# Fewer turns of P, a last stage by seven products, fewer pairs by rows, finer first pairs, and an order read from a table

## The chip, the core and the metric

The kernel runs on one core of a Trainium2 chip. Its metric is the device time of one execution, in microseconds. Five engines run their own instruction streams and wait for each other by semaphores: PE (TensorE: matmul and turns, that is, transposes by a product with the identity), ACT (ScalarE), DVE (VectorE), POOL (GpSimd), and SP, which here only issues DMAs (ACT and POOL issue some too).

## The reference

Inputs are q, k and v of shape (4, 12, 448, 64) and two weight matrices of 768 x 2048 and 2048 x 768, the weights as 64-bit floats. What is computed:

```python
scores = (q @ k.T) / 8, with the upper triangle masked          # 4 batches x 12 heads
attn = softmax(scores)
x = (attn @ v), heads side by side                              # 1792 tokens x 768
h = maximum(x @ w_in, 0)
out = (h * h) @ w_out                                           # 1792 x 768
```

## The kernel before, in words

Two heads of one batch make a **pair**; there are 24. For a pair, q and k are brought to a layout with the 64 head dimensions of both heads along 128 partitions. Most pairs are loaded in 32 x 14 x 32 blocks, eight DMAs for q and k, and DVE transposes 32 x 32 blocks (L403). Pairs 4 to 9 (`ROWS`) are loaded by rows, four DMAs, turned on PE (L389, eight turns a pair), and copied out of PSUM by ACT (L318) or DVE (L399).

The 448 queries of a pair are cut into seven chunks of 64; chunk c sees only its first 64(c+1) keys, so the widths are 64 to 448. Scores (L422) are written with one head in each half of the 128 partitions: each head's product uses 64 rows and 64 columns of the array. DVE adds the mask and takes the extreme of each row (L435), ACT takes the exponential and its sum (L439), DVE inverts the seven sums at once (L515, L516), and POOL or DVE scales P (L448, L450). Then P is turned in 128 x 128 blocks (L462). A chunk whose width is an odd multiple of 64 leaves its last block half empty, filled with zeros at the start (L263); so a pair takes 16 turns in four groups of four, each group one PSUM bank, copied to `pt` by ACT (L318) or DVE (L470). P times V (L482) gives x for two heads. In the names of tiles, a pair's tiles begin with `a` or `b` (even and odd pairs of the first twelve; all later pairs use `a`).

Every large matrix is held as a rounded part and a remainder, and each large product is three matmuls: high x high, high x low, low x high (L679 to L681 and L1098 to L1100 for the first 896 tokens, L860 to L864 and L986 to L988 for the second). The weights come as 64-bit words and are converted by ACT, DVE and POOL.

For the first 896 tokens (pairs 0 to 11), four groups of 512 of the 2048 hidden features go one after another: an h stage (x times w_in, ReLU, square), then an o stage (times w_out). Pairs 12 to 23 are computed meanwhile, and their x goes to memory. The second 896 tokens use a 2 x 2 split of each product with seven block products instead of eight; sums and differences of blocks are prepared by DVE, POOL, ACT and accumulating DMAs that POOL issues. Groups come in the order 0, 3, 2, 1 (`TURNS`). The last o stage, of group 1 (`o_last`), takes all eight block products, as 12 outputs of 12 matmuls; its outputs are added to the sums of earlier groups, transposed by DVE (L1036), and stored. The very last output is added in two parts (`finish`, L1063 to L1078).

The order is set by `Plan`: each `plan.op` has a rank, its engines with estimated times, and what it reads and writes. `emit` runs a list schedule over these estimates and writes the instructions of all engines in that order; `AMENDS` shifts ranks. [...]

Of the kernel before, what the change touches and what calls it, by code (L numbers as in the profile page):

```python
# [20 lines left out]
class Op:  # L21
    __slots__ = ("rank", "ways", "then", "left", "ready", "take", "drop", "lag", "bias")
# [14 lines left out]
class Plan:  # L37

    LAG = {PE: 0.25, ACT: 0.3, DVE: 0.3, POOL: 0.3, DMA: 0.5, DMA2: 0.5}
    ISSUE = 1.4
    BEGIN, BACKLOG = 1.3, 2.5
    FEW = {PE: 0.0, ACT: 0.5, DVE: 1.0, POOL: 0.0, DMA: 0.0, DMA2: 0.0}
    MANY = {PE: 0.0, ACT: 0.0, DVE: 0.3, POOL: 0.0, DMA: 0.0, DMA2: 0.0}

    def __init__(self):  # L50
# [21 lines left out]
    def op(self, rank, ways, reads=(), writes=(), after=(), take=None, drop=(), clear=(), lag=0.0):  # L72
        o = Op()
        o.rank, o.ways, o.then, o.ready, o.take, o.drop = rank, ways, [], 0.0, take, drop
        o.lag, o.bias = lag, self.bias
# [24 lines left out]
    def amend(self, table):  # L100
        for first, end, more in table:
            for o in self.ops[first:end]:
                o.rank += more

    def emit(self):
        free = [1.0, 1.9, 3.4, 2.7, 0.7, 0.7]
        ready = [o for o in self.ops if o.left == 0]
        order, port, net = [], 0.0, 0.0
        while ready:
            best = None  # L110
            for o in ready:
                at = o.ready + (self.ISSUE if o.ways[0][0] >= DMA else 0.0)
                if o.take:
                    h, n = o.take[0], len(o.take)
                    if self.held[h.kind] + n > self.caps[h.kind] or len(self.pools[h.pool]) < n:
                        continue
                    at = max(at, sorted(self.pools[h.pool])[n - 1][0])
                at += o.lag
                if o.ways[0][0] >= DMA:
                    at = max(at, net - self.BACKLOG)  # L120

                w = min(
                    (max(free[w[0]], at, port if shared(w) else 0.0) + w[1] + o.bias[w[0]],
                     max(free[w[0]], at, port if shared(w) else 0.0), i, w[0])
                    for i, w in enumerate(o.ways)
                )
                key = (w[1], o.rank)
                if best is None or key < best[0]:
                    best = (key, o, w)
            _, o, (_, start, i, e) = best  # L130
            ready.remove(o)
            free[e] = end = start + o.ways[i][1]
            if shared(o.ways[i]):
                port = max(port, end)
            if e >= DMA:
                net = max(net, start + self.BEGIN) + o.ways[i][3]
                end = max(end, net)
            order.append((start, len(order), o, i))
# [52 lines left out]
def kernel(  # L191
# [54 lines left out]
    ROWS, RB = range(4, 10), S // NK  # L246
# [4 lines left out]
    class Buffers:  # L251
        def __init__(s, nm, pool):
# [22 lines left out]
    mask = pool.tile([P, S], F32, name="mask")  # L275
# [18 lines left out]
    NX = 9  # L294
    wide = wi_t.rearrange("p i c f -> p (i c f)")
# [12 lines left out]
    for i in range(2):  # L308
        m = mask[i * QC:(i + 1) * QC, S - QC:]
# [34 lines left out]
    def attention(s, n, at):  # L344
# [956 lines left out]
```

## Time and profile before

| | us |
|---|---|
| median of 3 runs (lowest to highest) | 604.77 (604.64 to 605.73) |
| profiled execution, its own time | 606.17 |
| its span, from first to last instruction | 604.3 |
| PE busy | 587.0 (97% of the span) |
| DVE, ACT, POOL busy | 418.8, 361.8, 348.1 |
| mean granted clock of TensorE | 0.999 |

So 1.9 us of the profiled execution lie outside its span. Times below count from the start of the span. "Busy" is the union of an engine's instructions. [...]

### The profile page before, as it was taken

The page shows a single profiled execution, that of the slowest core. Times are in us where ns is not written, and L with a number is a line of the kernel's source. Part 1 is how long each engine was busy: PE and PEld are TensorE (multiplying, and loading weights), DVE is VectorE, ACT ScalarE, POOL GpSimd, SP SyncE. Part 2 cuts the span into 40 slices and gives each one's busy share as a digit, 9 for nine tenths or more (in the row PEclk, how much of TensorE's full clock was granted, in tenths as well). Part 3 has the DMA queues.
Part 4 walks back from the last instruction along what each step waited for, and adds up shares of the span by engine and source line. Part 5 has one row for each costly group of instructions (what it writes and reads, how often), then busy time and mean ns, then how long its engine had stood idle before and what let it go on. Part 6 is the DMA issues. An engine that isn't in the chain of part 4 may idle for free.

```text
span 604.3 us, 11456 instructions
## 1 busy us (share of the span) xinstructions
PE 587.0 (97%) x3766; PEld 513.8 (85%) x3766; DVE 418.8 (69%) x951; ACT 361.8 (60%) x889; POOL 348.1 (58%) x460
## 2 busy tenths in 40 slices
PE   3999999999999999999999999999999999999997
PEld 2677777898988998888898889998999899999996
DVE  4997976366985887775677616688782777777454
ACT  3889997665687656577447543367764573752400
POOL 2574673764585844867557754256685566777000
PEclk9999999999999999999999999999999999999999
DMA  9899745979789888987898759869868746771555
GB/s 148 168 204 179 165 103 116 257 232 329 191 208 315 247 238 217 282 232 226 255 242 259 268 189 263 274 188 238 207 152 163 195 116 135 158 177 41 183 92 93
DMA packets 190652, 120.02 MB, mean 199 GB/s; under 512 B 126016, under 2 KB 178560, under 8 KB 190592
## 3 DMA queue, kind: packets, MB, share of 16 engines
q1 hardware_dynamic: 169488, 107.99, 64.8%
q0 software_dynamic: 6912, 9.44, 10.0%
q10 hardware_dynamic: 14192, 1.85, 1.9%
q8 instruction: 30, 0.49, 0.3%
q14 instruction: 30, 0.25, 0.2%
HBM read 80.71 MB, written 38.54 MB: 197 GB/s over the span
## 4 chain that ended last, share of the span: by engine, by line
PE 90%; DMA 4%; ACT 2%; SPq 2%; issue 1%; DVE 0%; ACTq 0%; DVEq 0%
PE ps L1098 7%; PE ps L679 7%; PE ps L1100 6%; PE ps L1099 6%; PE ps L681 6%; PE ps L680 6%; PE ps L482 6%; PE ps L462 6%; PE ps L986 6%; PE ps L988 6%; PE ps L987 6%; PE ps L422 5%; PE ps L860 5%; PE ps L864 5%; PE ps L862 5%; DMA words<-in_moe_w_in_dram 2%
## 5 line engine op out<-in xcount | busy, mean ns | idle before, releaser
L318 ACT ACTIVATE words<-words 128x384 f32<-128x384 f32 (+3 forms) x140 | 79.8, 597 | 27.9 <-DVE words L321 15.3
L448 POOL TENSOR_SCALAR ap<-ap,asm 128x64 f32<-128x64 f32 (+6 forms) x123 | 74.6, 626 | 30.6 <-DVE asm L516 27.7
L435 DVE CUSTOM_DVE_ANT_0 ps<-ps,mask 128x448 f32<-128x448 f32 (+6 forms) x168 | 68.4, 446 | 19.2 <-PE ps L422 12.9
L1098 PE MATMUL ps<-wo,g 128*128 128x384 f32 x224 | 76.8, 343 | 0.0
L1100 PE MATMUL ps<-wo,g 128*128 128x384 f32 x224 | 75.1, 335 | 0.0
L1099 PE MATMUL ps<-wo,g 128*128 128x384 f32 x224 | 75.0, 335 | 0.0
L679 PE MATMUL ps<-x,wi 128*128 128x448 f32 x192 | 74.1, 386 | 0.6 <-ACT aqt L318 0.6
L681 PE MATMUL ps<-x,wi 128*128 128x448 f32 x192 | 70.3, 366 | 0.0
L680 PE MATMUL ps<-x,wi 128*128 128x448 f32 x192 | 70.3, 366 | 0.0
L439 ACT ACTIVATE ap<-ps,mx 128x448 f32<-128x448 f32 (+6 forms) x126 | 59.2, 487 | 15.0 <-DVE mx L435 11.1
L325 POOL TENSOR_TENSOR wi<-words,wi 128x384 fp32r<-128x384 f32 (+1 forms) x44 | 52.6, 1204 | 11.8 <-ACT wi L318 6.6
L860 PE MATMUL ps<-x,wi 128*128 128x448 f32 x156 | 57.3, 367 | 0.3 <-DMA wi<-wi_split 0.3
L318 ACT ACTIVATE r<-ps 128x448 f32<-128x448 f32 x60 | 32.5, 545 | 41.4 <-PE ps L681 17.5
L862 PE MATMUL ps<-x,wi 128*128 128x448 f32 x156 | 57.2, 367 | 0.0
L864 PE MATMUL ps<-x,wi 128*128 128x448 f32 x156 | 57.2, 367 | 0.0
L986 PE MATMUL ps<-g,wi 128*128 128x448 f32 x153 | 56.0, 366 | 0.3 <-DMA wi<-wo_split 0.3
L987 PE MATMUL ps<-g,wi 128*128 128x448 f32 x153 | 56.0, 366 | 0.0
L988 PE MATMUL ps<-g,wi 128*128 128x448 f32 x153 | 56.0, 366 | 0.0
L331 POOL TENSOR_SCALAR wi<-words 128x384 fp32r<-128x384 f32 (+1 forms) x39 | 26.9, 689 | 46.6 <-DVE words L643 23.0
L640 DVE TENSOR_SCALAR words<-words 128x384 int32<-128x384 int32 (+1 forms) x56 | 30.3, 543 | 23.2 <-ACT words L318 23.1
L321 DVE CUSTOM_DVE_ANT_0 words<-words 128x768 uint16<-128x768 uint16 (+1 forms) x56 | 42.3, 755 | 5.8 <-ACT words L318 3.3
L318 ACT ACTIVATE apt<-ps 128x512 f32<-128x512 f32 x65 | 35.6, 611 | 14.5 <-PE ps L462 14.4
(149 smaller groups left out, 1459.9 us busy)
## 6 DMA issues: line engine op xcount, KB each, us to landing
words<-in_moe_w_in_dram SPq DMA_DIRECT2D x24, 512.0 KB, 5.6
words<-in_moe_w_out_dram SPq DMA_DIRECT2D x32, 384.0 KB, 3.7
wo_split<-wo SPq DMA_DIRECT2D x26, 384.0 KB, 4.8
wi<-wo_split SPq DMA_DIRECT2D x24, 384.0 KB, 4.1
wo_whole<-words SPq DMA_DIRECT2D x32, 192.0 KB, 3.9
wi_split<-wi SPq DMA_DIRECT2D x24, 256.0 KB, 4.0
v<-in_v_dram SPq DMA_DIRECT2D x24, 192.0 KB, 4.1
wi_whole<-words SPq DMA_DIRECT2D x18, 256.0 KB, 4.0
```

The lines of the kernel that those rows point to most:

```text
L318: return (ACT, t_act(n, psum, more), lambda: nc.scalar.activation(dst(), src(), func, **kw))
L679: nc.tensor.matmul(o, w[:, 0], x[:, 0], start=c == 0, stop=False)
L680: nc.tensor.matmul(o, w[:, 0], x[:, 1], start=False, stop=False)
L681: nc.tensor.matmul(o, w[:, 1], x[:, 0], start=False, stop=c == NP - 1)
L860: nc.tensor.matmul(o, w.t[:, 0, c], x[:, 0], start=begin and c == 0, stop=False, skip_group_check=True)
L862: nc.tensor.matmul(o, w.t[:, 0, c], x[:, 1], start=False, stop=False, skip_group_check=True)
L986: nc.tensor.matmul(o, w.t[:, 0, d], g.t[:, 0], start=start, stop=False, skip_group_check=True)
L987: nc.tensor.matmul(o, w.t[:, 0, d], g.t[:, 1], start=False, stop=False, skip_group_check=True)
L988: nc.tensor.matmul(o, w.t[:, 1, d], g.t[:, 0], start=False, stop=stop, skip_group_check=True)
L1098: nc.tensor.matmul(res(), g[:, 0], w[:, 0], start=f == 0, stop=False)
L1099: nc.tensor.matmul(res(), g[:, 0], w[:, 1], start=False, stop=False)
L1100: nc.tensor.matmul(res(), g[:, 1], w[:, 0], start=False, stop=f == GF - 1)
```

## The change

- **Turns.** P of a pair is laid out without gaps, in the chunk order 1, 3, 5, 2, 0, 6, 4 (`ALONG`). The last 64 columns of chunks 2 and 0, and of 6 and 4, then lie side by side and are turned together (`TWINS`): 14 turns a pair instead of 16, in groups of 4, 4, 4 and 2. The group of two is copied out by two instructions of 64 partitions each. In `pt`, the half that such blocks don't fill is set to zero once.
- **Scores of chunk 4.** For this layout its last 64 keys stand first (`FIRST`); its product is written as two matmuls a head, of 256 and 64 columns, and the mask is wider.
- **Rows.** Only pairs 4 and 5 are loaded by rows; 6 to 9 come in blocks, with DVE transposes.
- **First pairs.** Pairs 0 and 1 take their scores in two or three groups with PSUM places of their own, and invert the sums of chunks 0 to 4 and of 5 and 6 apart.
- **Last o stage.** It takes seven block products instead of eight, each of 2 x 3 matmuls on three column blocks. The last pairs of h units therefore make the differences as the other groups do (`plain` is gone), the weights of the stage need the sums that accumulating DMAs build, and the second h pair of group 1 comes before the o stage of group 2. Buffers of x are reused for weights and h once the last h product has read them (`lent_x`).
- **Order.** `emit` no longer plans: each operation has a number in the table `PLACES`, which gives its place in one total order and, by its remainder, the engine.

```diff
+    def emit(self, table):
+        codes = [int(x, 36) for x in table.split()]
+        assert len(codes) == len(self.ops)
+        done = set()
+        for n, (code, o) in enumerate(sorted(zip(codes, self.ops), key=lambda x: x[0])):
+            assert all(d in done for d in o.deps)
...
+            o.ways[code % 3][2]()
...
+                    self.pools[h.pool].append((n + 1,) + h.tile)
+            done.add(o)
...
-    ROWS, RB = range(4, 10), S // NK
+    ROWS, RB = range(4, 6), S // NK
...
+    SOON = {6: (0, 0), 5: (1, 0), 4: (2, 0), 3: (3, 0), 1: (4, 0), 2: (5, 0), 0: (5, 3 * QC)}
+    NEXT = {**PLACE, 0: (3, 7 * QC)}
+    FAST = 2
...
+    ALONG = (1, 3, 5, 2, 0, 6, 4)
+    TWINS = ((2, 0), (6, 4))
+    POFF = {c: sum(CW[x] for x in ALONG[:i]) for i, c in enumerate(ALONG)}
+    FIRST = {4: QC}
...
+    QUADS = (
+        ((5, 0), (6, 0), (5, 1), (6, 1)),
+        ((1, 0), (2, 0), (3, 0), (4, 0)),
+        ((3, 1), (4, 1), (5, 2), (6, 2)),
+        TWINS,
+    )
...
-            for c in range(NQ):
-                if CW[c] < CK[c] * P:
-                    nc.vector.memset(s.p[:, POFF[c] + CW[c]:POFF[c] + CK[c] * P], 0.0)
+            for kc in range(NK):
+                nc.vector.memset(s.pt[QC:, TOFF[kc]:TOFF[kc] + P], 0.0)
...
-                        h = j ^ (PLACE[c][0] & 1)
-                        nc.tensor.matmul(
-                            place(c)[h * QC:(h + 1) * QC], s.qt[mine, c * QC:(c + 1) * QC],
-                            s.kt[mine, :CW[c]], start=True, stop=True, skip_group_check=True)
+                        h = j ^ (place_at[c][0] & 1)
+                        off = FIRST.get(c, 0)
+                        for k0, k1, to in ((0, CW[c] - off, off), (CW[c] - off, CW[c], 0)):
+                            if k0 < k1:
+                                nc.tensor.matmul(
+                                    place(c)[h * QC:(h + 1) * QC, to:to + k1 - k0], s.qt[mine, c * QC:(c + 1) * QC],
+                                    s.kt[mine, k0:k1], start=True, stop=True, skip_group_check=True)
...
-            blocks = TURNED[4 * i:4 * i + 4]
+            blocks = QUADS[i]
+            twins = blocks is TWINS
 
             def go():
                 for n, (c, kc) in enumerate(blocks):
+                    a = POFF[c] + CW[c] - QC if twins else POFF[c] + FIRST.get(c, 0) + kc * P
                     o = QC * (PLACE[c][0] & 1)
-                    nc.tensor.transpose(
-                        ps.t[:, n * P:(n + 1) * P],
-                        s.p[:, POFF[c] + kc * P:POFF[c] + (kc + 1) * P], ident[:, o:o + P])
-            plan.op(at, [(PE, 4 * 0.109, go)], [(nm, "p", c) for c, _ in blocks], [ps],
-                    take=ps, clear=[(nm, "pt", i)], lag=spare(1.6))
-            t = s.pt[:, 4 * i * P:4 * (i + 1) * P]
-            plan.op(at, [
-                on_act(512, lambda: t, lambda: ps.t, True),
-                (DVE, t_dve(512) + 0.05, lambda: nc.vector.tensor_copy(t, ps.t)),
-            ], [ps], [(nm, "pt", i)], drop=[ps])
+                    nc.tensor.transpose(ps.t[:, n * P:(n + 1) * P], s.p[:, a:a + P], ident[:, o:o + P])
+            plan.op(at, [(PE, len(blocks) * 0.109, go)],
+                    [(nm, "p", c) for c in sorted({c for b in blocks for c in (b if twins else b[:1])})], [ps],
+                    take=ps, clear=[(nm, "pt", i, h) for h in range(2)] if twins else [(nm, "pt", i)], lag=spare(1.6))
...
+            if twins:
+                for h in range(2):
+                    copied([(nm, "pt", i, h)], [(b[h], b[h] // 2) for b in blocks],
+                           slice(h * QC, (h + 1) * QC), slice(0, QC))
+            else:
+                copied([(nm, "pt", i)], blocks, slice(None), slice(None))
...
+        if fast:
+            groups = ((6, 5), (4, 3, 2, 1, 0)) if n else ((4, 3), (2, 1, 0), (6, 5))
...
+        for first, end in ((0, 5), (5, NQ))[::-1 if n else 1] if fast else ((0, NQ),):
+            def inverse(sums=s.sm[:, first:end]):
+                nc.vector.tensor_scalar(sums, sums, 1.0e-9, None, op0=ALU.add)
+                nc.vector.reciprocal(sums, sums)
+            keys = [(nm, "sm", c) for c in range(first, end)]
+            plan.op(at, [(DVE, 0.4, inverse) + SHARED], [], keys)
+            for c in range(first, end):
+                normalise(c, keys, at)
...
-        if plain:
-            factor("12", "12", True)
-            return rank
...
+    O_LAST = {"11": ("a", "11"), "12": ("b", "11"), "s2": ("a", "12"), "s1": ("c", "22"),
+              "s3": ("a", "22"), "s4": ("c", "12"), "22": ("a", "21")}
...
-        for k in ("11", "21", "12", "22"):
-            i, j = k
-            for d in range(CB):
-                ps, a = Hold("ps", "os"), o_sum(k, d)
-                rank = o_product(ps, [(W[i + m, u], g7[TURNS[-1], m + j, u]) for m in "12" for u in range(2)],
...
+        bank = {}
+        for d in range(CB):
+            for key, (b, k) in O_LAST.items():
+                begin = key in ("11", "12", "s1")
+                if begin:
+                    bank[b] = Hold("ps", "os")
+                ps, a = bank[b], o_sum(k, d)
+                rank = o_product(ps, [(W[key, u], g7[TURNS[-1], OTHER[key], u]) for u in range(2)],
+                                 d, begin, True, rank, step)
+                if (key, d) == ("22", CB - 1):
+                    finish(ps, k, d, rank)
                     continue
+                plan.op(rank, [on_dve(S, a, lambda ps=ps: ps.t[:, :S], a, ALU.add)], [ps], [("sum", k, d)],
+                        drop=[ps] if key in ("12", "22", "s4") else [])
+                if key in ("12", "22", "s3", "s4"):
+                    put_out(k, d, rank)
...
-        stages += [(a, 0) for a in after] + [(gr, None)] + [(a, 1) for a in after]
-    for gr, u in stages:
+        early_pair = after == TURNS[-1:]
+        stages += [(a, 0) for a in after] + [(a, 1) for a in after if early_pair]
+        stages += [(gr, None)] + [(a, 1) for a in after if not early_pair]
...
-    AMENDS = (
-        (0, 25, 5.5), (25, 31, 9.6), (31, 44, 13.9), (44, 61, 9.6), (61, 62, -25.2), (62, 65, -33.7),
...
-    plan.amend(AMENDS)
+    PLACES = """
+        00c 00l 00o 006 000 003 00i 00f 009 02o 066 07r 07o 00r 00x 02c 02x 030 043 04c 010 01u 020 01f 01x 01i 03r 016
...
```

What the table does to the engines is shown at three places. First PE, at the turns of pair 2 and the scores of pair 4 (`ap` is P of pair 2, `akt` and `aqt` the k and q of pair 4), before:

```order
L462 MATMUL ps_117<-ident,ap 128x128 x4
L462 MATMUL ps_118<-ident,ap 128x128 x4
L462 MATMUL ps_119<-ident,ap 128x128 x4
L462 MATMUL ps_116<-ident,ap 128x128 x4
L422 MATMUL ps_120<-akt,aqt 64x448 x2
L422 MATMUL ps_115<-akt,aqt 64x384 x2
L422 MATMUL ps_115<-akt,aqt 64x64 x2
L422 MATMUL ps_117<-akt,aqt 64x320 x2
L422 MATMUL ps_119<-akt,aqt 64x256 x2
```

and now:

```order
L425 MATMUL ps_117<-ident,ap 128x128 x4
L425 MATMUL ps_119<-ident,ap 128x128 x4
L425 MATMUL ps_113<-ident,ap 128x128 x4
L425 MATMUL ps_118<-ident,ap 128x128 x2
L383 MATMUL ps_116<-akt,aqt 64x448 x2
L383 MATMUL ps_120<-akt,aqt 64x384 x2
L383 MATMUL ps_120<-akt,aqt 64x64 x2
L383 MATMUL ps_114<-akt,aqt 64x256
L383 MATMUL ps_114<-akt,aqt 64x64
L383 MATMUL ps_114<-akt,aqt 64x256
L383 MATMUL ps_114<-akt,aqt 64x64
L383 MATMUL ps_119<-akt,aqt 64x256 x2
```

The last group of turns has two instead of four. Of chunk 4 (320 wide before) the two heads' matmuls no longer stand next to each other: one head's 256 and 64 come ahead of the other head's.

Second DVE, in the first pairs (`bkt` and `bqt` are k and q of pair 1, `asm` the sums of pair 0, ISA with `mask` the extremes of a chunk and `mx` their read-out), before:

```order
L435 ISA ps_115,mx_108<-ps_115,mask 128x320
L435 ISA mx_108 128x1
L435 ISA ps_116,mx_109<-ps_116,mask 128x256
L435 ISA mx_109 128x1
L435 ISA ps_116,mx_110<-ps_116,mask 128x192
L435 ISA mx_110 128x1
L435 ISA ps_115,mx_111<-ps_115,mask 128x128
L435 ISA mx_111 128x1
L403 STREAM_TRANSPOSE bkt<-bk 128x448
L403 STREAM_TRANSPOSE bqt<-bq 128x448
L515 TENSOR_SCALAR asm<-asm 128x7
L516 RECIPROCAL asm<-asm 128x7
```

and now:

```order
L358 STREAM_TRANSPOSE bqt<-bq 128x448
L396 ISA ps_116,mx_108<-ps_116,mask 128x384
L396 ISA mx_108 128x1
L358 STREAM_TRANSPOSE bkt<-bk 128x448
L396 ISA ps_117,mx_109<-ps_117,mask 128x320
L396 ISA mx_109 128x1
L396 ISA ps_115,mx_110<-ps_115,mask 128x448
L396 ISA mx_110 128x1
L503 TENSOR_SCALAR asm<-asm 128x2
L504 RECIPROCAL asm<-asm 128x2
L396 ISA ps_119,mx_111<-ps_119,mask 128x320
L396 ISA mx_111 128x1
```

Pair 1's transposes moved from behind all seven chunks of pair 0 to among them (three narrow chunks stand ahead of this piece), and two sums of pair 0 are inverted before pair 0's chunk of 256, which comes later.

Third DVE at the end of the program (`sb` are sums of outputs, L1036 and now L1034 the transposes ahead of the stores), before:

```order
L321 TENSOR_TENSOR sb_4316<-ps_113,sb_4316 128x448
L1036 STREAM_TRANSPOSE words<-sb_4316 128x448
L321 TENSOR_TENSOR sb_4317<-ps_115,sb_4317 128x448
L1036 STREAM_TRANSPOSE words<-sb_4317 128x448
L321 TENSOR_TENSOR sb_4318<-ps_118,sb_4318 128x256
```

and now:

```order
L276 TENSOR_TENSOR sb_4366<-ps_118,sb_4366 128x448
L276 TENSOR_TENSOR sb_4366<-ps_115,sb_4366 128x448
L1034 STREAM_TRANSPOSE words<-sb_4366 128x448
L276 TENSOR_TENSOR sb_4372<-ps_118,sb_4372 128x448
L1034 STREAM_TRANSPOSE words<-sb_4372 128x448
L276 TENSOR_TENSOR sb_4369<-ps_119,sb_4369 128x448
L276 TENSOR_TENSOR sb_4369<-sb_4369,sa_3859 128x448
L276 TENSOR_TENSOR sb_4369<-ps_118,sb_4369 128x256
```

Each block product of six matmuls now has an addition of its own, where an output of twelve matmuls had one. Of the five block products in this piece the fourth (`sb_4369<-ps_119`) is one of group 2's o stage, and an addition of two sums stands behind it.

## Rows read from the trace of the kernel before

**Rows 1.** The page: PE in 40 slices of the span, busy tenths.

```profile
PE   3999999999999999999999999999999999999997
```

**Rows 2.** Windows: stretch, then busy us (instructions) of PE, PEld, DVE, ACT, POOL; clock, DMA.

```profile
0.00:20.00 20.00, 9.44 (x94) 6.32 (x97) 11.41 (x48) 8.81 (x31) 5.51 (x18) 1.00 0.90 150
20.00:50.00 30.00, 28.13 (x269) 20.59 (x262) 26.95 (x88) 27.13 (x85) 20.08 (x35) 1.00 0.95 189
20.00:106.00 86.00, 84.13 (x787) 62.42 (x781) 70.92 (x237) 76.96 (x237) 52.17 (x93) 1.00 0.75 156
60.00:70.00 10.00, 10.00 (x94) 7.33 (x94) 9.46 (x36) 9.86 (x32) 7.70 (x15) 1.00 0.85 204
350.00:590.00 240.00, 239.43 (x1206) 221.05 (x1205) 160.18 (x261) 117.94 (x235) 128.50 (x149) 1.00 0.68 172
```

**Rows 3.** Waits of PE: line, waited for: us in total, times, longest.

```profile
PE ps L422 <- DVE aqt L403: 7.3, 2, 6.7
```

**Rows 4.** Timeline of PE, 57 to 70 us: start, us, line, tiles, shape, count.

```profile
57.24 0.93 PE L389 MATMUL ps<-ident,rows 112*128 112x112 f32 x8
58.11 1.83 PE L422 MATMUL ps<-bkt,bqt 64*64 64x448 f32 x28
...
65.64 1.75 PE L422 MATMUL ps<-akt,aqt 64*64 64x448 f32 x28
67.32 1.95 PE L482 MATMUL ps<-apt,v 128*64 128x448 f32 x16
```

**Rows 5.** Timeline of PE, first and last of 120 matmuls in the last stage.

```profile
574.80 0.36 PE L986 MATMUL ps<-g,wi 128*128 128x448 f32 x1
...
598.92 0.37 PE L988 MATMUL ps<-g,wi 128*128 128x448 f32 x1
```

**Rows 6.** Timeline of DVE at the end: additions and a transpose.

```profile
596.89 0.62 DVE L321 TENSOR_TENSOR sb<-ps,sb 128x448 f32<-128x448 f32 x1 [1.13 <-PE ps L988]
597.55 0.65 DVE L1036 STREAM_TRANSPOSE words<-sb 128x448 f32<-128x448 f32 x1
```

**Rows 7.** Timeline of PE in narrow windows: scores of one pair, chunk by chunk.

```profile
65.64 0.59 PE L422 MATMUL ps<-akt,aqt 64*64 64x448 f32 x4
66.03 0.58 PE L422 MATMUL ps<-akt,aqt 64*64 64x384 f32 x4
66.45 0.43 PE L422 MATMUL ps<-akt,aqt 64*64 64x320 f32 x4
```

**Rows 8.** Timeline of the first 30 us: pairs 0 and 1.

```profile
6.73 3.27 PE L422 MATMUL ps<-akt,aqt 64*64 64x448 f32 x28 [6.73 <-DVE aqt L403]
8.64 0.63 DVE L435 CUSTOM_DVE_ANT_0 ps<-ps,mask 128x448 f32<-128x448 f32 x1 [1.89 <-PE ps L422]
12.00 0.64 DVE L403 STREAM_TRANSPOSE bkt<-bk 128x448 f32<-128x448 f32 x1
13.22 3.10 PE L422 MATMUL ps<-bkt,bqt 64*64 64x320 f32 x28 [3.22 <-DVE asm L515]
16.25 1.99 PE L462 MATMUL ps<-ident,ap 128*128 128x128 f32 x16
```

**Rows 9.** Groups of DVE by form, 0 to 106 us: count, busy us, mean ns.

```profile
L403 DVE STREAM_TRANSPOSE akt<-ak 128x448 f32<-128x448 f32 x5 | 3.2, 642 | 4.0 <-DMA ak<-in_k_dram 4.0
L470 DVE COPY apt<-ps 128x512 f32<-128x512 f32 x5 | 3.4, 679 | 0.0
L321 DVE TENSOR_TENSOR wi<-words,wi 128x512 fp32r<-128x512 f32 x2 | 1.4, 686 | 0.0
L399 DVE COPY aqt<-ps 128x448 f32<-128x448 f32 x1 | 0.6, 610 | 0.0
L450 DVE TENSOR_SCALAR bp<-bp,bsm 128x384 f32<-128x384 f32 x1 | 0.5, 480 | 0.0
```

**Rows 10.** Timeline at 107 us: POOL and DVE side by side.

```profile
107.68 1.15 POOL L325 TENSOR_TENSOR g<-r,g 128x448 fp32r<-128x448 f32 x1
...
107.86 1.17 DVE L450 TENSOR_SCALAR ap<-ap,asm 128x320 f32<-128x320 f32 x1
```

More of the change, by code (lines that the diff above doesn't have):

```diff
@@ L21 @@
 class Op:
-    __slots__ = ("rank", "ways", "then", "left", "ready", "take", "drop", "lag", "bias")
+    __slots__ = ("rank", "ways", "take", "drop", "deps")
 class Hold:
@@ L37 @@
 class Plan:
[L44 to L48, printed above, removed]
     def __init__(self):
@@ L93, in op @@
                 self.readers.setdefault(k, []).append(o)
-        o.left = len(deps)
-        for d in deps:
-            d.then.append(o)
+        o.deps = deps
         self.ops.append(o)
         return o
[L100 to L138, printed above, removed]
+    def emit(self, table):
[4 more added lines that the diff above has]
+            assert all(d in done for d in o.deps)
             for h in o.take:
@@ L274 @@
     ident = pool.tile([P, 3 * QC], F32, name="ident")
[L275 removed]
+    mask = pool.tile([P, S + CW[4] - QC], F32, name="mask")
     even = Buffers("a", pool)
@@ L486, in times_v @@
             plan.op(at, [(PE, 0.2 + 4 * sum((S - kc * P) / 2400 for kc in range(NK)), go)],
-                    [(vr, kc) for kc in range(NK)] + [(nm, "pt", i) for i in range(len(TURNED) // 4)], [av], take=av, drop=[vr],
+                    [(vr, kc) for kc in range(NK)] + KEYS, [av], take=av, drop=[vr],
                     lag=spare(1.0))
@@ L865, in go @@
                                      skip_group_check=True)
-                plan.op(rank, [(PE, 3 * t_mm(S), go)],
-                        [(w, 0), (w, 1)] + [(("x7", OTHER[key], c), i) for i in range(2)], [ps],
-                        take=ps if begin and c == 0 else None, drop=[w])
+                used.setdefault(OTHER[key], []).append(plan.op(
+                    rank, [(PE, 3 * t_mm(S), go)],
+                    [(w, 0), (w, 1)] + [(("x7", OTHER[key], c), i) for i in range(2)], [ps],
+                    take=ps if begin and c == 0 else None, drop=[w]))
                 rank += step
@@ L946, in o_parts @@
     def o_parts(gr, rank, last):
-        W, Z, gate = {}, {}, list(ahead)
+        W, Z, gate, order = {}, {}, list(ahead), tuple(O_LAST) if gr == TURNS[-1] else SEVEN
         def at(key, u):
-            return rank + (last - rank) * (SEVEN.index(key) + u / 2) / 7
+            return rank + (last - rank) * (order.index(key) + u / 2) / 7
         def flat(t):
@@ new lines, in o_last, with put_out, go @@
+        return rank
+    def put_out(k, d, rank):
+        i, j = k
+        a, h = o_sum(k, d), Hold("f", "tr")
+        plan.op(rank, [(DVE, t_dve(S) + 0.05, lambda: nc.vector.transpose(h.t, a()))],
+                [("sum", k, d)], [h], take=h)
+        row, col = T + (int(j) - 1) * S, (int(i) - 1) * CH + d * P
+        for s in range(P // SQ):
+            def go(eng, s=s):
+                return lambda: eng.dma_start(
+                    out=out[row:row + S, col + s * SQ:col + (s + 1) * SQ].rearrange(
+                        "(b p) d -> p b d", p=SQ),
+                    in_=h.t[s * SQ:(s + 1) * SQ].rearrange("p (b d) -> p b d", d=SQ))
+            plan.op(rank, [(DMA, 0.6, go(nc.sync), t_dma(S, 128)), (DMA2, 0.6, go(nc.scalar), t_dma(S, 128))], [h], [], drop=[h])
@@ L1063, in turn @@
                     nc.tensor.transpose(turned.t[:n, m - first:m - first + P], a()[:, m:m + n], late["ident"])
-            plan.op(rank, [(PE, 0.22, turn)], [("sum", "22", d, first)], [turned], take=turned)
+            plan.op(rank, [(PE, 0.22, turn)], [("sum", k, d, first)], [turned], take=turned)
             blocks = [(0, 2, P)] if first == 0 else [(0, 1, P), (1, 1, S - 3 * P)]
```

245 lines of the change are left out of this document (179 added, 66 removed), and 47 rows, old and new, of the table AMENDS.

## The prediction

> **What bounds the kernel now.** I read the page first, for the engine that has no time left. PE is 97% busy, and its row of 40 slices shows 9 in all but the first and the last [rows 1]. By the windows it sits idle for 10.6 us in the first 20 us, for 1.9 us up to 50 us, and for 0.6 us between 350 and 590 us [rows 2]. The waits of PE name the cause: two waits for DVE's transposes of q, 7.3 us [rows 3], and one of 3.2 us that is put down to the sums [rows 8]. So the end is set by the sum of PE's work plus the start, and a part of the change is worth what PE no longer does, as long as no other engine takes over. The candidate is DVE: it is busy for 70.9 of 86 us from 20 to 106 us, where the first twelve pairs run, and for 160 of 240 us later on [rows 2].
>
> The sum is made against the profiled execution: 604.3 us of span and 1.9 us around it, 606.2 us. That is 1.4 us above the median of the runs, 604.8, and the difference that I work out is taken from the median.
>
> **Fewer turns.** Eight turns take PE from 57.24 to 58.11 us, 0.109 us each [rows 4] (those are of rows; turns of P have the same width of weights). 24 pairs lose two each: 48 x 0.109 = 5.2 us. The two copies of 64 partitions that replace one copy of 512 columns lie on ACT and DVE and cost PE nothing where these keep up; DVE is counted below.
>
> **Rows.** Pairs 6 to 9 lose eight turns each: 32 x 0.109 = 3.5 us. Their loads are now eight DMAs in blocks instead of four, and two DVE transposes.
>
> **Last o stage.** 120 matmuls from 574.80 to 598.92 us are 119 steps of 0.203 us [rows 5]. The stage has 144 matmuls and will have 126: 18 x 0.203 = 3.65 us. Its extra preparation (differences of four blocks for two h pairs, sums of weights by accumulating DMAs) goes to DVE, POOL and ACT, which are a half to two thirds busy in that stretch [rows 2]: I cost it at nothing, and what it costs if it comes late is a rival. DVE's additions and transposes end last: 0.62 us and 0.65 us for a product [rows 6], 1.27 us, against 6 x 0.203 = 1.22 us of PE. That trails by tenths at the end, 0.1 us.
>
> **Scores of chunk 4, a cost.** Scores of a pair take 1.68 us, from 65.64 to 67.32 us [rows 4]. [...] The narrow windows show how: all four records of the 448 wide chunk start at 65.64 us, those of the 384 wide one from 66.03 us on, when the first has run through [rows 7]. [...] Now a head's 64 columns stand between its 256 and the other head's 256. [...] That is 0.19 us a pair, 24 x 0.19 = 4.6 us. [...] I take 4.6, since in [rows 7] no chunk starts ahead of the one before it.
>
> [...]
>
> **First pairs, a gain.** PE starts at 6.73 us, when the transposes of pair 0 are done; that stays. DVE then takes seven chunks from 8.64 to 12.00 us, transposes k and q of pair 1 behind them, and PE gets to pair 1 at 13.22 us; the turns of pair 0 come at 16.25 us [rows 8]. Now three narrow chunks and the 384 wide one stand ahead of the end of these transposes: 768 of 1792 columns, 768 / 1792 x 3.36 = 1.4 us, plus the two transposes, 1.2 us (12.00 to 13.22 us), and DVE can begin some 0.6 us sooner since the first group of scores is 384 columns wide and not 448 and more. 8.6 - 0.6 + 1.4 + 1.2 = 10.6 us instead of 13.2. I take 2.5 us. The bounds are nothing (what follows is bound by ACT and DVE anyway) and all the idle time between 6.73 and 20 us, 20 - 9.44 - 6.73 = 3.8 us [rows 2].
>
> **DVE in the first twelve pairs, a new wait.** I counted DVE's stream up to the last remainder of x in both orders. It gains 8 transposes at 0.64 us, 5.1 us; 10 copies of half a block, between half of 0.68 us and the whole, I take 0.42 us, 4.2 us; 15 scalings that POOL did, at some 0.4 us by the 0.48 us of the one of 384 columns, 6.0 us; two more inverses, 0.8 us. It loses four copies of turned rows at 0.61 us, two remainders of weights at 0.69 us and one of h: 4.4 us [rows 9]. In sum 11.7 us more. Some 2 us of it fall before 20 us, where DVE has room. So DVE has 70.9 + 11.7 - 2 = 80.6 us to do after 20 us. PE alone would reach the end of this stretch earlier by 24 x 0.109 + 3.5 - 12 x 0.19 + 2.5 = 6.3 us, which leaves DVE 79.7 us. It can't be 101% busy; the densest ten microseconds of before are at 94.6% [rows 2], and by that share it needs 85.2 us. PE, whose stream has the order fixed, would wait for the difference, 5.5 us. The other bound is nothing: two transposes of 0.64 us each take 1.2 us together, so that the list counts overlapping ends of records, and not all of this is awaited. I take 2.4 us, a little under the middle.
>
> A wait of DVE can be read too: a scaling on DVE took 1.17 us where others take 0.48, while POOL ran an operation of two inputs [rows 9, 10]. [...]
>
> **Sum.** -5.2 - 3.5 - 3.65 + 4.6 - 2.5 + 2.4 + 0.1 = -7.8 us. 604.8 - 7.8 = 597.0 us.
>
> **Rivals.**
> - *The split is free and DVE keeps up.* PE's work falls by 5.2 + 3.5 + 3.65 - 0.7 and the start by 2.5: 14.2 us, 590.6 us. For it: PE hides everything for 500 us now [rows 1]. [...]
> - *The new order waits in the late stages.* Each block product of the last stage needs a weight that comes by DMA, accumulation, and two conversions, and an h that comes through four subtractions. If some are late, PE stops in order; 3 to 8 us in all would give 600 to 605 us, 602 the likeliest. Against it: PE now waits for 0.6 us in 240 there [rows 2], with the same kind of parts for three groups.
> - *Slower: DVE sets the pace of the first twelve pairs.* If DVE stays at the share that it has now, 70.9 / 86 = 82%, its 80.6 us take 97.7 us, 18 us more than PE leaves it; then -10.3 + 18 = +7.7 us, 612.5 us. It decides from a share under 88%: 80.6 / 0.88 = 91.6 us, 11.9 us over, which eats the gain and 0.2%. For it: DVE waits for PE and ACT in turn, and ACT is busy for 77 of 86 us in the same stretch [rows 2]. Against it: part of DVE's idle time now is there because PE is the slower one.
>
> **Chances and range.** Within 0.2%, 1.2 us, a measurement of this kernel tells no change. Forecast (593.5 to 600) 0.52, faster; free split 0.23, faster; late waits 0.16, of which 0.12 faster and 0.04 no change; slow DVE 0.09, of which 0.08 slower. So faster 0.87, same 0.05, slower 0.08. The range reaches from 589.5, a little under the free split, to 602.5, the likely late waits; outside are the worse waits and most of the slow DVE, under 0.2.
>
> **What would show it.** Right: PE's L383 takes about 1.87 us a pair instead of 1.68, with a gap in which only one head runs; groups of two turns 0.22 us shorter than groups of four; the second scores near 10.6 us; the first twelve pairs done some 4 us sooner; PE's new waits in the first 100 us are for DVE (scaling, extremes, transposes); after 110 us PE is busy throughout. Wrong: scores still at 1.68 us; waits of PE for weights or h in the last 60 us; or DVE waiting for POOL in most scalings.

## The result, and the profile after

The changed kernel takes 609.25 us (median of 4 runs, 608.71 to 611.44) against 604.83 us before: ratio 1.0087, 95% interval 1.0072 to 1.0103. It is 0.9% slower, where I had forecast 597.0. The profiled execution took 608.96 us, with a span of 606.9 us (before 604.3). So the two traces lie 2.6 us apart where the medians lie 4.4 apart; what is read from the traces below explains the former.

The windows of after, columns as in [rows 2], have two of the stretches shown there, and two late ones:

```profile
0.00:20.00 20.00, 10.29 (x92) 7.19 (x96) 12.69 (x55) 11.11 (x35) 7.26 (x21) 0.90 0.91 157
20.00:106.00 86.00, 84.15 (x798) 61.35 (x791) 77.28 (x262) 76.51 (x239) 46.35 (x79) 0.98 0.74 152
540.00:560.00 20.00, 19.05 (x93) 16.83 (x92) 18.94 (x26) 12.58 (x26) 12.89 (x16) 1.00 0.78 197
560.00:570.00 10.00, 5.29 (x20) 4.44 (x19) 8.47 (x11) 1.57 (x3) 3.86 (x5) 0.83 0.44 109
```

The last row is new: PE works 5.29 of 10 us at a mean clock of 0.83, where in before it was busy throughout:

```profile
560.00:570.00 10.00, 10.00 (x51) 9.24 (x50) 3.13 (x6) 3.68 (x7) 1.13 (x2) 1.00 0.68 215
```

The waits of PE, where [rows 3] had one long one, name DVE there:

```profile
PE ps L383 <- DVE aqt L358: 6.8, 1, 6.8
PE ps L973 <- DVE sb L276: 4.7, 1, 4.7
PE ps L425 <- POOL ap L409: 2.9, 3, 1.6
PE ps L973 <- DVE r L276: 0.7, 1, 0.7
```

Counting the matmuls of the block products in the timeline of PE tells when the time went. All pairs are done by 540 us in both. There after has passed 20 more of them than before and has 18 fewer to do in all: 38 x 0.203 = 7.7 us ahead, just the forecast. From there before needs 64.3 us for 291 matmuls, after 66.9 us for 253: 10.3 us lost in the last 66. They are 5.7 us of idle PE from 540 to 570 us, 1.5 us at a granted clock of 0.50 behind it (565.60 to 568.75 us), and 2.0 us in the end (from the last product's end to the span's 7.1 us, before 5.0). A wait also costs PE more than its idle time (4.87 us for the idle 4.71 at 560 us). By steps from one record's start to the next, each against 0.203 us (in [rows 5] records of 0.36 to 0.37 us begin 0.203 us apart), the first two come to 8.0 us: 6.4 at one stall at 560 us with its half clock, 1.6 at two waits at 541 to 544 us. That leaves 0.3 us.

**The stall.** The timeline of after, first PE, then DVE, at 556 us (the like of [rows 10], and larger):

```profile
560.53 0.37 PE L975 MATMUL ps<-x,wi 128*128 128x448 f32 x1
565.60 0.74 PE L973 MATMUL ps<-g,wi 128*128 128x448 f32 x1 [4.71 <-DVE sb L276]
568.38 0.55 PE L974 MATMUL ps<-x,x 128*128 128x448 f32 x1
568.75 0.38 PE L975 MATMUL ps<-x,x 128*128 128x448 f32 x1
```

```profile
555.37 0.61 DVE L276 TENSOR_TENSOR r<-r,r 128x448 f32<-128x448 f32 x1
556.39 6.39 DVE L276 TENSOR_TENSOR g<-r,g 128x448 fp32r<-128x448 f32 x1 [0.42 <-ACT g L273]
562.71 0.61 DVE L276 TENSOR_TENSOR sb<-ps,sb 128x448 f32<-128x448 f32 x1
```

One subtraction took 6.39 us where the median of this form on DVE is 0.62 in this trace (in e2_warm, below, PE again waits 4.8 us for DVE's sums), and the sums that free PSUM banks for PE stood behind it. In that time POOL worked through this without a gap:

```profile
556.19 0.87 POOL L730 DMA_DIRECT2D f<-wo_whole  x1 [1.47 <-ACT f L273]
556.75 1.35 POOL L280 TENSOR_TENSOR x<-words,x 128x384 fp32r<-128x384 f32 x1
557.74 0.83 POOL L286 TENSOR_SCALAR x<-words 128x384 fp32r<-128x384 f32 x1
558.22 1.33 POOL L280 TENSOR_TENSOR wi<-words,wi 128x384 fp32r<-128x384 f32 x1
559.20 1.32 POOL L280 TENSOR_TENSOR x<-words,x 128x384 fp32r<-128x384 f32 x1
560.17 1.29 POOL L280 TENSOR_TENSOR wi<-words,wi 128x384 fp32r<-128x384 f32 x1
561.14 0.84 POOL L286 TENSOR_SCALAR g<-f 128x448 fp32r<-128x448 f32 x1
561.65 1.18 POOL L730 DMA_DIRECT2D words<-wo_whole  x1
```

DVE's instruction ends at 562.78 us; by its usual 0.62 us it would have begun at 562.16, just after POOL's last operation ended (561.14 + 0.84 = 561.98).

### The profile page after: what moved, and what is told of

Read it like the earlier page. It is cut to its first block, busy times and chain, and to the rows that moved or that the text cites. A ratio compares the mean times of both kernels' runs of the same rounds, so it can differ in the third digit from the quotient of the medians.

```text
span 606.9 us, 11517 instructions
## 1 busy us (share of the span) xinstructions
PE 583.3 (96%) x3764; PEld 510.6 (84%) x3764; DVE 473.8 (78%) x1085; ACT 356.9 (59%) x899; POOL 306.5 (51%) x403
## 4 chain that ended last, share of the span: by engine, by line
PE 85%; DVE 6%; ACT 4%; issue 2%; DMA 1%; POOL 1%; DVEq 0%; ACTq 0%
PE ps L1096 7%; PE ps L1097 6%; PE ps L1098 6%; PE ps L667 6%; PE ps L668 6%; PE ps L669 6%; PE ps L848 6%; PE ps L850 6%; PE ps L852 6%; PE ps L467 5%; PE ps L973 5%; PE ps L974 5%; PE ps L975 5%; PE ps L425 5%; PE ps L383 5%
## 5 line engine op out<-in xcount | busy, mean ns | idle before, releaser
L396 DVE CUSTOM_DVE_ANT_0 ps<-ps,mask 128x256 f32<-128x256 f32 (+6 forms) x168 | 68.0, 445 | 15.9 <-PE ps L383 13.7
L409 POOL TENSOR_SCALAR ap<-ap,asm 128x448 f32<-128x448 f32 (+6 forms) x86 | 47.0, 561 | 60.2 <-DVE asm L504 31.6
L400 ACT ACTIVATE ap<-ps,mx 128x384 f32<-128x384 f32 (+6 forms) x126 | 58.7, 475 | 28.3 <-DVE mx L396 28.1
L667 PE MATMUL ps<-x,wi 128*128 128x448 f32 x192 | 73.4, 382 | 0.0
L280 POOL TENSOR_TENSOR wi<-words,wi 128x384 fp32r<-128x384 f32 (+1 forms) x46 | 57.5, 1258 | 25.6 <-ACT wi L273 24.5
L668 PE MATMUL ps<-x,wi 128*128 128x448 f32 x192 | 70.3, 366 | 0.0
L669 PE MATMUL ps<-x,wi 128*128 128x448 f32 x192 | 70.3, 366 | 0.0
L848 PE MATMUL ps<-x,wi 128*128 128x448 f32 x150 | 55.1, 367 | 0.2 <-DVE r L276 0.2
L850 PE MATMUL ps<-x,wi 128*128 128x448 f32 x150 | 55.1, 367 | 0.0
L852 PE MATMUL ps<-x,wi 128*128 128x448 f32 x150 | 55.0, 367 | 0.0
L273 ACT ACTIVATE wi<-words 128x384 fp32r<-128x384 f32 (+1 forms) x53 | 28.7, 550 | 39.7 <-PE ps L974 13.7
L276 DVE TENSOR_TENSOR g<-r,g 128x448 fp32r<-128x448 f32 x49 | 42.8, 879 | 8.5 <-ACT g L273 6.9
L973 PE MATMUL ps<-g,wi 128*128 128x448 f32 x108 | 40.5, 375 | 5.4 <-DVE sb L276 4.7
L383 PE MATMUL ps<-akt,aqt 64*64 64x64 f32 (+5 forms) x576 | 37.1, 385 | 7.4 <-DVE aqt L358 6.8
L1096 PEld LDWEIGHTS ps<-wo,g 128*128 128x128 f32 x224 | 42.1, 188 | 0.9 <-issue 0.2
L1097 PEld LDWEIGHTS ps<-wo,g 128*128 128x128 f32 x224 | 42.1, 188 | 0.4
L1098 PEld LDWEIGHTS ps<-wo,g 128*128 128x128 f32 x224 | 42.1, 188 | 0.0
```

Of the source, the lines that this page charges most:

```text
L273: return (ACT, t_act(n, psum, more), lambda: nc.scalar.activation(dst(), src(), func, **kw))
L396: plan.op(at, [(DVE, t_dve(w), lambda: nc.vector.tensor_tensor_reduce(out=at_(), in0=at_(), in1=mask[:, S - (FIRST.get(c) or w):][:, :w], ...
L667: nc.tensor.matmul(o, w[:, 0], x[:, 0], start=c == 0, stop=False)
L668: nc.tensor.matmul(o, w[:, 0], x[:, 1], start=False, stop=False)
L669: nc.tensor.matmul(o, w[:, 1], x[:, 0], start=False, stop=c == NP - 1)
L848: nc.tensor.matmul(o, w.t[:, 0, c], x[:, 0], start=begin and c == 0, stop=False, skip_group_check=True)
```

## The experiments

Each is an edit of the changed kernel, or of e5_lock3 where that is said, and is timed against before on the same chip; times are medians, with the ratio to before and its interval. The medians of before on these chips lie between 604.66 and 605.51 us, so differences under 1 us between experiments say nothing.

**e1_lock: four of POOL's subtractions in that run go to DVE.**

```diff
+    moved = (gr, key, u) in ((2, "s4", 1), (2, "s4", 0), (1, "s2", 0), (1, "s1", 0))
-    ... take=w, ways=OWAY)
+    ... take=w, ways=slice(0, 1) if moved else OWAY)
```

> Four subtractions of the last stage's weight parts (128x384, 0.97 us apart on GpSimd) go from GpSimd to VectorE; in the changed kernel they stood in an unbroken run on GpSimd from 556.75 to 561.98 us, beside which one subtraction on VectorE took 6.39 us where its like takes 0.62. Theory A (VectorE's instruction could not start while GpSimd ran on without a gap; the wait is the run's): that subtraction takes under 1.5 us, TensorE's wait of 4.71 us at 560.9 is gone and the stretch at half clock behind it (9 products at 0.37 instead of 0.205 us, 1.5 us) as well, VectorE pays 4 x 0.47 = 1.9 us in places where it has room: 609.25 - 4.7 - 1.5 = about 603, 602 to 605. Rival B (VectorE is simply full there, busy 97 % of 530 to 550 us): it has 1.9 us more to do, the wait grows, 609 to 611.

605.81 us, 1.0005 (0.9991 to 1.0019). The subtraction that had been held and one of those moved (DVE), then PE's new wait:

```profile
556.97 0.93 DVE L276 TENSOR_TENSOR g<-r,g 128x448 fp32r<-128x448 f32 x1 [0.50 <-ACT g L273]
563.14 0.54 DVE L276 TENSOR_TENSOR wi<-words,wi 128x384 fp32r<-128x384 f32 x1
```

```profile
563.74 0.47 PE L976 MATMUL ps<-g,wi 128*128 128x448 f32 x1 [1.87 <-DVE wi L276]
```

B falls: DVE has more to do and the kernel is 3.4 us faster than after. A has the cause right and the time too low: one of the moved subtractions now comes late on DVE.

**e5_lock3: that one back on POOL** (`(2, "s4", 0)` leaves the list).

> The last stage once more, now with three of the four subtractions on VectorE: the one whose result TensorE waited 1.87 us for at 561.9 us in e1_lock (the s4 part of group 2, made by VectorE at 563.14) goes back to GpSimd, which is idle from 558.2 to 559.1 there. Theory A (a VectorE instruction is held only while GpSimd runs on without a gap, so two or three GpSimd instructions cost it that much and not 5.8 us): that wait goes, VectorE has no instruction over 2.5 us there, 605.8 - 1.9 = 603.9, 603.3 to 604.6. Rival B (any GpSimd subtraction there holds VectorE up again and the product sums come late): no better than e1_lock, 605.5 to 607.

603.72 us, 0.9983 (0.9971 to 0.9995): A, to 0.2 us, and the first version that is ahead of both kernels, of before by 0.17%. PE's longest wait from 545 us to the last product is now

```profile
562.09 0.48 PE L974 MATMUL ps<-g,wi 128*128 128x448 f32 x1 [0.48 <-DVE sb L276]
```

In this run DVE and POOL still meet (1.84 us for a subtraction of a form that took 0.54 in e1_lock), and DVE gets in sooner:

```profile
557.93 1.84 DVE L276 TENSOR_TENSOR x<-words,x 128x384 fp32r<-128x384 f32 x1
```

```profile
557.48 0.90 POOL L286 TENSOR_SCALAR x<-words 128x384 fp32r<-128x384 f32 x1
558.36 1.00 POOL L280 TENSOR_TENSOR wi<-words,wi 128x384 fp32r<-128x384 f32 x1
559.34 0.86 POOL L286 TENSOR_SCALAR g<-f 128x448 fp32r<-128x448 f32 x1
```

It ended at 559.77 us, so by its usual 0.54 us it would have begun at about 559.23, when the two-input operation was ending (559.36), with no gap on POOL behind it. A's "only while POOL runs on without a gap" is thus too strong; at which boundary DVE gets in stays open. That POOL's run is the cause is shown (the subtraction held for 6.39 us in after takes 0.93 in e1_lock and 0.90 here), and what breaking it up gave: 609.25 - 603.72 = 5.5 us (6.3 by the two ratios). In steps of PE from 540 us on it is 8.0 us lost in after and 2.5 in e5_lock3.

**e2_warm: PE kept at work in its two early waits.**

```diff
...
+    for _ in range(extra):      # pair 0: 8 ahead of its group 0, 12 ahead of group 2
+        nc.tensor.transpose(ps.t[:, :P], ident[:, :P], ident[:, :P])
```

> Twenty dummy turns of the identity (0.109 us each) ahead of the first pair's first turns, 8 and 12 of them, into banks that the true turns then overwrite: TensorE works through what were its two waits of 0.94 and 1.57 us at 13.1 and 14.8 us; nothing else is changed and the turns wait for the same scalings. Theory A (the granted clock of 0.50 from 16 to 22.7 us follows from these waits): the clock stays at 1.00, the third pair's scores (3.28 us) take about 1.8 and the first product with V starts 2 to 3 us before 24.05; of these 3 us the end gets between 0.5 and 3, since VectorE and ScalarE set the pace of the first twelve pairs: 606 to 609, 607.5 likeliest. Rival B (the clock falls for another reason): the same stretch still runs at 0.50, no change or up to 0.3 us slower.

609.76 us, 1.0072 (1.0054 to 1.0091): no gain that can be told from after's 1.0087 (1.0072 to 1.0103). The windows of after, then of e2_warm:

```profile
16.00:18.00 2.00, 1.65 (x7) 1.36 (x8) 1.36 (x7) 1.85 (x6) 1.13 (x4) 0.50 0.84 147
20.00:22.00 2.00, 2.00 (x28) 1.19 (x20) 1.32 (x7) 0.90 (x3) 1.10 (x3) 0.50 0.73 119
```

```profile
16.00:18.00 2.00, 1.56 (x13) 1.10 (x10) 1.54 (x7) 1.82 (x8) 1.24 (x3) 1.00 0.95 161
20.00:22.00 2.00, 2.00 (x28) 1.57 (x20) 1.94 (x9) 1.54 (x6) 1.28 (x4) 1.00 0.96 146
```

A is right on the clock: it stays at 1.00, the third pair's scores take 1.76 us instead of 3.28, the first product with V starts at 22.57 instead of 24.05 us. It is wrong on the end: of these 1.5 us 0.4 are left at the third product with V (36.03 against 36.39 us), and the twelfth ends at 105.63 against 105.91. In between PE waits for others: for a copy of turned P on DVE before that third product (0.72 us), and for 0.98 us at 28.6 us for what the profile puts down to a load of q.

**e4_unsplit: chunk 4's scores whole.**

```diff
-    for k0, k1, to in ((0, CW[c] - off, off), (CW[c] - off, CW[c], 0)):
+    for k0, k1, to in ((0, CW[c], 0),):
```

> Chunk 4's scores by one product of 320 columns a head instead of 256 and 64 (its columns then stand in the order of before, so that chunk's turns read other columns than they should: for the time alone). The trace has a pair's scores at 1.80 us against 1.75 before, where I had forecast 1.87 against 1.68. Theory A (that difference is the whole cost): 24 x 0.05 = 1.2 us less at most, 608.0 to 609.2. Rival B (my forecast, 0.19 a pair): 4.6 us less, about 604.7.

609.7 us, 1.0075 (1.0057 to 1.0092). B falls. A's 1.2 us are 0.2%, too little to be told by these two intervals; in the trace the scores of the twelve later pairs take 1.68 us again, from the first one's start to the next instruction of PE, where after has 1.72 or 1.73.

**e7_short, e9_loads: less work for DVE, less to load.**

```diff
+    w = SQ if n in range(6, 10) else S
-    nc.vector.transpose(dst, src)
+    nc.vector.transpose(dst[:, :w], src[:, :w])        # e7_short
-    nc.sync.dma_start(out=raw.t[:, :n], in_=src)
+    nc.sync.dma_start(out=raw.t[:, :m], in_=src[:, :m])   # e9_loads
```

> The eight transposes of q and k on VectorE of pairs 6 to 9, which the change moved there from TensorE's rows, done for 32 of 448 columns only (the other columns keep what the pair before left: for the time alone): 8 x some 0.5 = 4 us less on VectorE between 50 and 90 us. Theory A (VectorE, ScalarE and the chain through them set the pace of the first twelve pairs, so what the rows took off TensorE came back as VectorE's): the twelfth product with V ends 2 to 4 us before 105.91, the end 2 to 4 us earlier: 605.5 to 607.3. Rival B (TensorE's own work, or ScalarE or the loads, set it): under 1 us, 608.5 to 609.3.

> The changed kernel, the six loads of group 0's input weights (512 KB each, 3 of the 9.1 MB that move from 8 to 60 us) cut to a quarter of their columns; the rest of those words stays zero, so the products of that group are not the reference's: for the time alone. Theory A (the loads set the pace of pairs 2 to 7: the transfer engines are 88 to 90 % busy from 8 to 60 us before as after): 2.25 MB less at some 180 GB/s is 12 us of transfers, so q and k arrive earlier and the twelfth product with V ends 2 to 5 us before 105.91; the end 604 to 607. Rival B (the chain score, maximum, exponential, sum, scaling, turn, copy, product on the engines' fixed orders sets it): under 1 us, 608.4 to 609.6.

610.26 us (1.0083, 1.0065 to 1.0102) and 610.48 us (1.009, 1.0077 to 1.0103); the twelfth product with V ends at 105.72 and 106.00 us. Group 0's weight loads don't set the pace of the first pairs, and neither does DVE's work where e7_short takes it away. But that is 2.8 us of busy DVE from 20 to 106 us (74.45 instead of 77.28), and only 0.65 of it before 52 us.

**e8_pool, e11_dve: scalings moved either way.** Digits of the table alone, here one each:

```diff
-... 05a ...    # e8_pool: way 1 of 13 scalings, DVE
+... 059 ...    # way 0, POOL
-... 056 ...    # e11_dve: way 0 of 12 others, POOL
+... 057 ...    # way 1, DVE
```

> The 13 scalings of the first twelve pairs that VectorE does (L411, 0.34 us each, about 4.5 us) go to GpSimd (0.6 to 0.7 us each; it is 50 % busy there). Theory A (VectorE's load sets the pace): 1 to 3 us earlier, 606.5 to 608.3. Rival B (the length of one pair's chain sets it, and GpSimd's scaling is longer): the turns wait longer for scalings, no change or up to 2 us slower, 609 to 611.

> e5_lock3 with one scaling more of each of the first twelve pairs (the last that GpSimd does in the pair) on VectorE: 12 x some 0.35 us more on VectorE, 12 x some 0.5 us less on GpSimd. Moving 13 the other way made the kernel 5 us slower (614.7). Theory A (GpSimd's scalings stand in each pair's chain to its turns, and that chain sets the pace): 1 to 4 us faster than e5_lock3, 600 to 602.7. Rival B (the balance found by the table is the best near by, VectorE's own work is next in the chain): no change or slower, 603.4 to 606.

614.7 us (1.0156, 1.0135 to 1.0176), and 608.86 us (1.0063, 1.0051 to 1.0075), 5.1 us above e5_lock3, on which it builds. B both times, and worse than B said. The twelfth product with V begins at 108.41 us instead of 103.96, and at 109.99 instead of 104.55. What fits these four runs, without being shown by them, is that the chain of a pair through the engines' fixed streams sets the pace: work that is taken away beside it gives nothing, and a move of scalings to either engine makes it longer.

**e3_tail, e6_lane, e10_gps, e12_few: the stores at the end.** The two last stores on ACT; one store on ACT; three stores of e5_lock3 on POOL; six stores of e5_lock3 left out.

```diff
-    (DMA, 0.4, store(nc.sync), ...) if first else
+    (DMA2, 0.4, store(nc.scalar), ...) if first else   # e3_tail
-... 83u ...
+... 83v ...                                            # e6_lane
-    go(nc.sync)
+    go(nc.gpsimd if (k, d) in (("12", 2), ("22", 2)) else nc.sync)   # e10_gps
+    if (k, d) in (("21", 1), ("11", 2)) and s: return lambda: None   # e12_few
```

> The two last stores of the output go to ScalarE's queue instead of SP's. Theory A (they stood behind four earlier stores on SP that were issued from 601.06 to 603.03 us): they are issued at 601.9 to 602.9 instead of 603.13 to 604.29 and the end comes 1.2 us earlier: 608.0, 607.6 to 608.4. Rival B (the transfers themselves bound the end, so a store that is issued earlier only waits in its ring): no change, 609.0 to 609.4.

> One store of the changed kernel (the one that SP issued at 600.54 us, after standing 5.3 us at a store of ScalarE's queue, although its data were ready before 594) goes to ScalarE's queue: one digit of the table. [...] Theory A (this wait is what makes the end late: last product to end 7.05 us against 5.01 before): SP's last four stores are issued as their data come, the end comes 1.2 to 2 us earlier, 607.2 to 608.0. Rival B (the 27 stores of the last 15 us against 19 before fill the queues anyhow): 608.8 to 609.5.

> e5_lock3 with the three SP stores of the last two whole output tiles issued by GpSimd, which has nothing to do after 592 us. In e5_lock3 SP issues four stores from 596.12 to 598.12 and the two last from 598.46, and the end is 6.3 us after the last turn against 4.5 before. Theory A (SP's queue of stores at the end costs those 1.8 us): the two last stores are issued at 596.8 to 597.8, 1 to 1.6 us earlier: 602.1 to 602.7. Rival B (transfers of 128-byte rows fill the engines, or a store waits for another in any case): 603.4 to 604.2.

> e5_lock3 without six of the eight stores of two late output tiles (their rows stay unwritten: for the time alone). Theory A (the number of stores at the end, 27 issued in the changed kernel's last 17 us against 19 in the same stretch before, makes the end late): the end comes about 4.5 to 5 us after the last turn instead of 6.3, 602.0 to 602.7. Rival B (the last tile's own chain, turn, copy, store and landing, is the end whatever stands ahead): no change, 603.3 to 604.1.

609.72 us (1.0077, 1.0061 to 1.0092), 609.49 us (1.0072, 1.0054 to 1.009), 603.87 us (0.9981, 0.9969 to 0.9993), 602.66 us (0.996, 0.9945 to 0.9974). The first three are B. SP's timeline in after shows what I had gone by:

```profile
594.93 0.32 SPq L1039 DMA_DIRECT2D out_dram<-words  x1
600.54 0.32 SPq L1039 DMA_DIRECT2D out_dram<-f  x1
601.06 1.97 SPq L1039 DMA_DIRECT2D out_dram<-words  x4
603.13 1.16 SPq L1076 DMA_DIRECT2D out_dram<-words  x2
```

With the digit changed SP stood 5.2 us at another store instead. With POOL's help SP was through 2.4 us after the last turns began, where in e5_lock3 it took 3.8, and the last store landed 4.3 us after them instead of 5.2; but 1.8 us instead of 1.1 passed from there to the end. Only fewer stores help, as A said for e12_few: it ends 5.3 us after the last turns began, e5_lock3 6.3. So about 1 us of the 2.0 is the number of late stores; the rest stays open.

## Why the prediction was wrong

**The step that failed** is "its extra preparation ... I cost it at nothing". The totals that I gave for it (DVE and POOL half to two thirds busy over 240 us) say nothing about two engines that meet: the seven-product form brought POOL a run of weight subtractions beside DVE's subtractions of h, and one of these, held for 6.39 us, cost PE 6.4 us (stall and half clock). My second rival, late waits of 3 to 8 us, is what happened; with the late stores it came to some 10 us, and 597 + 10 would be 607. Without that stall e5_lock3 is still 6.7 us above the forecast.

Of meetings of DVE and POOL I had read one, a scaling that took 1.17 us on DVE beside an operation of POOL [rows 10], and the forecast has no term for it. Here one wait lasted through seven of POOL's instructions, 6.39 us. That POOL's run held DVE is shown, by 0.93 and 0.90 us where the run is broken up (e1_lock, e5_lock3); by what means is not.

**Last o stage, fewer turns, rows.** -12.35 us were forecast. The counts are those: 504 matmuls of L973 to L975 against 522, 14 turns a pair, rows for two pairs.

**Scores of chunk 4: +4.6 us forecast, some 0.7 us measured.** From one pair's scores to the next instruction of PE, the timeline of after has 1.69 us, against 1.68 in [rows 4]:

```profile
64.87 1.76 PE L383 MATMUL ps<-akt,aqt 64*64 64x256 f32 x32
66.56 1.95 PE L467 MATMUL ps<-apt,v 128*64 128x448 f32 x16
```

That is 0.01 us for this pair, and 0.04 to 0.05 for each of the twelve later ones (1.72 or 1.73 us), where I had 0.19. The forecast's 0.19 us a pair, 24 x 0.19 = 4.6 us, is a term that no run shows (it also stands in the 6.3 us by which PE was to be earlier in the first twelve pairs); what the runs show in its place is 0.01 to 0.05 us a pair, close to my first rival's 0.7 us for 24 pairs, which had no run behind it either. What I had wrong is the reading of [rows 7]: a row of the timeline merges instructions of one line and the same tiles, and shows the shape of the first. By shape, the four records of before that start from 65.64 to 65.67 us, and all that start in after from 80.70 to 81.18 us, are

```profile
L422 PE MATMUL ps<-akt,aqt 64*64 64x448 f32 x2 | 0.6, 587 | 0.0
L422 PE MATMUL ps<-akt,aqt 64*64 64x384 f32 x2 | 0.5, 533 | 0.0
```

```profile
L383 PE MATMUL ps<-akt,aqt 64*64 64x256 f32 x8 | 0.7, 402 | 0.0
```

So four products, two heads of two chunks, run side by side, and the 384 wide chunk had not waited for the 448 wide one. In after, chunk 4's 256 columns run beside chunk 3, which is 256 wide too. Both heads' 256 columns begin by 80.74 us and the first 64 at 81.19, though in the order under "The change" one head's 64 stand ahead of the other head's 256: that 256 did not wait behind the 64. My 4.6 us had assumed that it would; the trace does not agree with that, as far as PE got the stream in that order.

**First pairs and DVE's wait: -2.5 + 2.4 forecast, about +4 measured** (what is left of -7.7 us at 540 when -12.35 and the split are taken off). The second scores came at 10.48 us, as forecast (10.6). But what followed did not:

```profile
10.48 2.66 PE L383 MATMUL ps<-bkt,bqt 64*64 64x256 f32 x32 [0.34 <-DVE bkt L358]
14.09 0.66 PE L425 MATMUL ps<-ident,ap 128*128 128x128 f32 x4 [0.94 <-POOL ap L409]
16.32 2.69 PE L425 MATMUL ps<-ident,ap 128*128 128x128 f32 x10 [1.57 <-POOL ap L409]
18.95 3.28 PE L383 MATMUL ps<-akt,aqt 64*64 64x256 f32 x32
24.05 1.95 PE L467 MATMUL ps<-apt,v 128*64 128x448 f32 x16
```

Before, the third pair's scores had begun as early, so the gain was gone there:

```profile
18.85 1.75 PE L422 MATMUL ps<-akt,aqt 64*64 64x320 f32 x28 [0.61 <-DVE aqt L403]
```

The turns waited for scalings, the clock fell to 0.50, and the twelfth product with V ended 0.8 us earlier (105.91 against 106.69 us), not 4. Most of the time was lost before 52 us. When the fifth product with V begins (51.99 us, before 52.34), after has done 9 matmuls of the first h stage where before had done 18, and 22 turns fewer: 9 x 0.203 + 22 x 0.109 = 4.2 us less work in 0.35 us less time. So 3.9 us were lost there where 2.5 were to be gained. e2_warm shows that the clock alone was not what held it, e9_loads that the weight loads were not. e7_short took its work off DVE for the most part behind 52 us: there "DVE's share" was the wrong quantity. From 20 to 52 us DVE is busy for 29.02 of 32 us, and whether its share counts there stays open.

Where PE spent most of the lost time can be read. Groups of scores begin before their PSUM banks are free, as in after

```profile
35.29 0.97 PE L383 MATMUL ps<-akt,aqt 64*64 64x256 f32 x12 [0.60 <-DVE apt L447]
42.17 2.54 PE L383 MATMUL ps<-bkt,bqt 64*64 64x448 f32 x32
48.35 2.90 PE L383 MATMUL ps<-akt,aqt 64*64 64x448 f32 x32
71.33 2.24 PE L383 MATMUL ps<-bkt,bqt 64*64 64x256 f32 x32
```

where the same pairs of before, the first of them aside (2.04 us), have

```profile
42.35 1.75 PE L422 MATMUL ps<-bkt,bqt 64*64 64x320 f32 x28
50.66 1.75 PE L422 MATMUL ps<-akt,aqt 64*64 64x448 f32 x28
72.36 1.75 PE L422 MATMUL ps<-bkt,bqt 64*64 64x448 f32 x28
```

With the first (33.13 to 36.26 us) that is 10.8 us against 7.3, 3.5 more (3.8 in e4_unsplit, so not by the split). In the three groups without a mark of idle time, single records begin 0.05 to 0.06 us after an instruction that reads PSUM has ended: at 42.40 after a copy on ACT (42.34), at 43.74 after one on DVE (43.68), at 49.00 after an exponential on ACT (48.95), at 49.79 and 50.27 after copies on ACT (49.74, 50.22), at 72.59 after one on DVE (72.54). So PE waits there for PSUM that ACT and DVE have not yet read. The forecast has no term for that, and why they come later than before stays open.

**Tail: +0.1 forecast, +2.0 measured**; about half of it by the number of late stores.

The two early errors (split 3.9 too dear, first pairs some 4 too cheap) cancelled: that after was just the forecast ahead at 540 us was luck.

## What to carry to other kernels

Read busy shares engine by engine only for work that can wait. Where DVE and POOL both run operations from SBUF to SBUF, lay their streams side by side and look for a stretch in which POOL has several in a row: here one DVE subtraction caught there took 6.39 us, and PE waited 4.71 us for a sum behind it. After a change, look first for single instructions that took many times their usual duration (here 6.39 us against 0.62). And before you read an order from a merged row of a timeline, ask for its instructions by shape.

## What was not expected of the hardware

A DVE subtraction was held for 6.39 us beside POOL's run (0.93 and 0.90 us in e1_lock and e5_lock3, where the run is broken up), while in the kernel before no two-input operation of DVE took over 2.33 us. PE's clock fell to 0.50 after waits of 0.94 and 1.57 us with four turns between them, and stayed there from 16 to 22 us, though PE was busy for 5.65 of these 6 us; before, one wait of 3.22 us passed at 1.00 [rows 2, 8]. Twenty dummy turns in these waits kept it at 1.00 from 16 to 22 us, and the end did not move (609.76 against 609.25 us). Score products of 64 rows and 64 columns ran four at a time, two heads of two chunks (starts from 65.64 to 65.67 us before, each lasting 0.53 us or more), and a later one did not wait for an earlier one on other rows (80.74 against 81.19 us).
